# First output product by channels instead of by tokens; the last 64 channels kept as two token halves; x2 split straight from PSUM

## The chip, the cores and the metric

The kernel runs on one core of a Trainium2 chip. The metric is the device time of one execution in microseconds (us): lower is better. The engines are called as in the profile: PE is TensorE (PEld its weight loads), DVE is VectorE, ACT is ScalarE, POOL is GpSimd, SP the engine that issues most DMAs.

## What is computed

```python
# x (2, 4096, 192) f32; weight (8, 7); two pairs w_in (192, 2048), w_out (2048, 192) in f64; a (4), b (2)
w = softmax(weight)                       # per head, over 7 taps
x = causal_conv(x, w)                     # 7 taps along the tokens, head = 24 channels
h = x @ w_in1;  g = h * sigmoid(1.702 * h);  x2 = g @ w_out1
h = x2 @ w_in2
g = (a0 + a1*h + a2*h**2 + a3*h**3) / (1 + |b0|*|h| + |b1|*h**2 + 1e-6)
out = g @ w_out2
```

## The kernel before, in words

The 8192 tokens are 16 blocks of T = 512. Between the two matmul chains every value is channel- or feature-major: partitions are channels, columns are tokens. The 192 channels of a block stand as two tiles of 128 rows: the first 128 channels, and the last 64 channels **twice** (rows 0 to 63 and again 64 to 127), so that two 64-row products can be paired.

f32 products are made of f16 parts: an operand is scaled by a power of two and split into a high and a low half (`high` on ACT, `low` on DVE), and a product is three f16 matmuls (high by high, low by high, high by low). `h_product(m, n, i)` makes 2 x 128 features for 512 tokens of block n and layer m: 6 matmuls of 512 columns over 128 rows (L371) and 6 over 64 rows (L381), which go to two row halves of the array and two PSUM banks in turn. `o1_product` makes x2 = g @ w_out1 **by tokens**: 128 tokens are the stationary operand and 192 channels the columns (L403), 192 matmuls a block. x2 then has to be turned: `x2_natural` copies it from PSUM (ACT, three instructions, L449 and L451), `transposes` turns it on PE (8 times 128x128, L250), DVE takes its maximum (L456), `all_max` spreads that over the partitions with a small matmul (L82), DVE makes a power of two of it (`scales`), and `x2_split` writes the two f16 halves. `o2_chunk` is the last product in f32, 16 chunks a block.

The main loop runs phases j = 0 to 14, written out by hand: each engine executes its instructions in the order of the code. `front_phase` holds, for i = 0 to 7, one `h_product` of layer 1 for block j+1 (followed by GELU on ACT, `g1_high` on POOL, `g1_low` on DVE), one of layer 2 for block j (followed by `unit`: ACT, ACT, DVE, DVE, then `denominator` on DVE), a late `quotient` of block j-1, and two late `o2_chunk`s. `back_phase` holds the transposes of x for block j+3 and its convolution on POOL (`x_conv_pool`: two TENSOR_SCALAR, L297, and one TENSOR_TENSOR, L301, per tap), `o1_product`, the eight logs on ACT, and then what this document calls **the seam**: x2 of block j+1 from PSUM to its f16 halves, beside the inverses (ACT, L502), the first four quotients (DVE, L506) and three chunks of o2. To have work in the seam PE makes the first `h_product` of block j+2 early. PSUM gives three two-bank tiles in turn to the h products, the transposes and the small maxima, and one to each output product.

The 1/(1+q) of the rational function is sigmoid(-ln q), so ACT loads another table three times a phase. The prologue decodes and splits the f64 weights and handles block 0 (its output product in f32, `o1_whole`); blocks 0 to 2 are convolved by matmuls on PE (L286). `last_phase` is the front of block 15 alone.

Of the kernel before, what the change touches and what calls it, by code (L numbers as in the profile page):

```python
# [15 lines left out]
P = 128  # L16
# [4 lines left out]
def kernel(  # L21
# [24 lines left out]
    HALO = K - 1  # L46
    xf = x.rearrange("b s d -> (b s) d")
# [13 lines left out]
    wr = [const.tile([P, 2, DFF // 2], F16, name=f"wr{m}") for m in range(2)]  # L61
# [191 lines left out]

    def x_transpose(n):
        pt = ps_tile("pt")
        transposes(pt, xn_t.pop(n))
        keep = tiny.tile([P, 2, HALO], F32, tag="keep", name="keep")
        if n * T % S == 0:
            nc.gpsimd.memset(keep, 0.0)
            if n:  # L260
                xt_t.pop(n - 1)
        else:
            nc.gpsimd.tensor_copy(out=keep, in_=xt_t.pop(n - 1)[:, :, T:T + HALO])
        t = p1.tile([P, 2, HALO + T], F32, tag="xt", name="xt")
        nc.gpsimd.tensor_copy(out=t[:, :, 0:HALO], in_=keep)
        nc.scalar.activation(out=t[:, :, HALO:HALO + T], in_=pt, func=ACTF.Copy)
        xt_t[n] = t

# [14 lines left out]

    def x_conv_matmul(n, m):
        j, k = m // K, m % K
        nc.tensor.matmul(  # L286
            out=xc_t[n][:, j], lhsT=diag[j, k], rhs=xt_t[n][:, j, k:k + T], start=(k == 0), stop=(k == K - 1)
        )

    def x_conv_pool(n, k):  # L290
        t = xt_t[n]
# [4 lines left out]
        for j in range(2):  # L296
            nc.gpsimd.tensor_scalar(  # L297
                out=d[:, j], in0=t[:, j, k:k + T], scalar1=wt[:, j, k:k + 1], scalar2=1.0, op0=ALU.mult, op1=ALU.mult
            )
        if k:  # L300
            nc.gpsimd.tensor_tensor(out=c, in0=c, in1=d, op=ALU.add)  # L301

    def high(src, s, xs):
        nc.scalar.activation(out=xs[:, 0:2], in_=src, func=ACTF.Identity, scale=s)  # L304

    def low(src, s, xs):
        nc.vector.scalar_tensor_tensor(  # L307
            out=xs[:, 2:4], in0=src, scalar=s, in1=xs[:, 0:2], op0=ALU.mult, op1=ALU.subtract
# [17 lines left out]
    def x_red(n):  # L326
# [3 lines left out]
            out=red[:, 0:1], in_=xn_t[n][:, :, 0:D], axis=AX.XY, op=ALU.max, apply_absolute_value=True  # L330
# [18 lines left out]
    def x_scale_out(n):  # L349
        sc = sc1_t[n]  # L350
        mul(sc[:, 5:6], sc[:, 0:1], cst[:, 2:3])

    def x_high(n):
        xs = xs_t[0, n] = p2.tile([P, 4, T], F16, tag="xs1", name="xs1")
# [6 lines left out]
    def h_product(m, n, i):  # L361

        ph = ps_tile("ph")
        xs = xs_t[m, n]
        terms = ((0, 0), (1, 0), (0, 1))

        def main(first):
            for k in range(2):
                f = slice((NS * k + i) * P, (NS * k + i + 1) * P)
                for q, (a_, b_) in enumerate(terms):  # L370
                    nc.tensor.matmul(  # L371
                        out=ph[:, k], lhsT=wm[m][:, a_, f], rhs=xs[:, 2 * b_], start=(first and q == 0),
                        stop=(not first and q == 2),
                    )

        def rest(first):
            f = slice(i * P, (i + 1) * P)
            for q, (a_, b_) in enumerate(terms):
                for k in range(2):
                    rows = slice(k * D2, (k + 1) * D2)  # L380
                    nc.tensor.matmul(  # L381
                        out=ph[:, k], lhsT=wr[m][rows, a_, f], rhs=xs[rows, 2 * b_ + 1], start=(first and q == 0),
                        stop=(not first and q == 2),
                    )

        for part, first in (((main, True), (rest, False)) if m == 0 else ((rest, True), (main, False))):
            part(first)
        return ph

    po_t, o_done = {}, {}  # L390

    def o_chunk(m, n, f, terms, groups=range(NG)):
# [15 lines left out]
    def o1_product(n, i, hl):  # L408
        for k in range(2):
            f, ts = NS * k + i, slice(k * T, (k + 1) * T)  # L410
            gh, gl, wh, wl = hl[:, 0, ts], hl[:, 1, ts], wo1[:, f, 0:D], wo1[:, f, D:2 * D]
            o_chunk(0, n, f, ((gh, wh), (gh, wl), (gl, wh)))

    def o2_chunk(n, i, k, groups=range(NG)):
        pp = units_t[n][i][0]
        o_chunk(1, n, NS * k + i, ((pp[:, k * T:(k + 1) * T], wo2[:, NS * k + i]),), groups)
# [24 lines left out]
    def x2_natural(n, unit=None):  # L441
        po = po_t.pop((0, n))
        sc = sc1_t.pop(n)
        if unit is None:
            unit = sc[:, 5:6]
        t = p1.tile([P, NG, 2 * P], F32, tag="x2n", name="x2n")
        src = po[:, :, 0:2 * D].rearrange("p k (g d) -> p k g d", g=2)
        dst = t.rearrange("p (k g) d -> p k g d", k=2)
        nc.scalar.activation(out=dst[..., 0:P], in_=src[..., 0:P], func=ACTF.Identity, scale=unit)  # L449
        for c in (P, D):  # L450
            nc.scalar.activation(out=dst[..., c:c + D2], in_=src[..., P:D], func=ACTF.Identity, scale=unit)  # L451
        return t

    def x2_red(t):
        red = tiny.tile([P, 1], F32, tag="red2", name="red2")
        nc.vector.tensor_reduce(out=red, in_=t[:, :, 0:D], axis=AX.XY, op=ALU.max, apply_absolute_value=True)  # L456
        return red
# [8 lines left out]
    def x2_scales(sc):  # L466

        s = sc[:, 2:3]
        mul(s, sc[:, 0:1], cst[:, 3:4])
# [75 lines left out]
    late_pe, early = [], {}  # L545

    def last_phase(j):
# [24 lines left out]
        quotients(range(first))  # L572
        store(j - 1)
        units(first), units(first + 1)
# [13 lines left out]
    def front_phase(j, n1, extras):  # L588

        splits = []  # L590
        for i in range(NS):
            g = gelu(n1, early.pop((n1, i), None) or h_product(0, n1, i))
            hl = g1_high(n1, g)
            splits.append(hl)
            unit(j, h_product(1, j, i))
# [11 lines left out]
    def x2_split(n, pt, sc):  # L607
        xs = xs_t[1, n] = p2.tile([P, 4, T], F16, tag="xs2", name="xs2")
        high(pt, sc[:, 1:2], xs)
        low(pt, sc[:, 1:2], xs)  # L610
        x2_scales(sc)

    def back_phase(j, n1, n2, conv, splits):

        if conv is not None:
            x_transpose(conv)
            for k in range(K):
                x_conv_pool(conv, k)
        for i in range(NS):
            o1_product(n1, i, splits[i])  # L620
            log(j, i)
            if conv is not None and i == 5:
                x_max(conv)
# [208 lines left out]
```

## Time and profile before

| | |
|---|---|
| median of 3 runs | 1261.98 us (1261.32 to 1263.13) |
| the profiled execution: its own time, its span | 1262.34 us, 1260.5 us |
| busy, share of the span: PE, DVE, ACT, POOL | 96%, 84%, 68%, 48% |
| granted TensorE clock, mean | 0.996 of full speed |

A matmul's recorded duration holds its way through the array, which overlaps with the next one's; what a stream of matmuls costs is read from start to start. So "x16, 2.76 us" with a mean of 0.33 us for one is a stream in which one starts every (2.76 - 0.33) / 15 us. An f32 product of 192 columns leaves two records.

### The profile page before, as it was taken

What the parts mean: (1) busy time and instruction counts of PE and PEld (TensorE: products, weight loads), DVE (VectorE), ACT (ScalarE), POOL (GpSimd) and SP (SyncE); (2) the same over time, 40 slices, a digit from 0 to 9 for tenths busy, and PEclk for the clock granted to TensorE, in tenths of its full rate; (3) what the DMA queues carried; (4) which work ended last, traced back from release to release, by engine and by line L of the source; (5) the groups of instructions that cost most, each with busy time, mean ns of one, the idle gap of its engine ahead of it and who ended that gap; (6) DMA issues with size and microseconds to landing.
All of it is one profiled execution on the core that took longest, in us unless ns stands there. A gap on an engine that the chain in (4) does not pass through costs nothing.

```text
span 1260.5 us, 19971 instructions
## 1 busy us (share of the span) xinstructions
PE 1211.6 (96%) x8538; PEld 852.6 (68%) x8538; DVE 1062.8 (84%) x1048; ACT 860.2 (68%) x857; POOL 601.3 (48%) x429
## 2 busy tenths in 40 slices
PE   5899999999999999999999999999999999999997
PEld 2474766768676676867667686766768576686767
DVE  6877889797979979797997979889797988959685
ACT  2624866758586685867668586766858677594975
POOL 2023673928467392755739285572927548101000
PEclk9899999999999999999999999999999999999999
DMA  7700001001010100101010010101001000000000
GB/s 233 234 1 17 1 1 30 1 1 31 1 30 1 30 1 1 30 1 31 1 30 1 1 31 1 30 2 30 1 1 30 1 14 1 14 1 1 14 1 25
DMA packets 31162, 28.56 MB, mean 23 GB/s; under 512 B 9825, under 2 KB 30305, under 8 KB 30305
## 3 DMA queue, kind: packets, MB, share of 16 engines
q1 hardware_dynamic: 30480, 27.27, 7.5%
q8 instruction: 67, 1.10, 0.4%
q14 instruction: 22, 0.18, 0.1%
q10 hardware_dynamic: 593, 0.01, 0.0%
HBM read 20.98 MB, written 6.29 MB: 22 GB/s over the span
## 4 chain that ended last, share of the span: by engine, by line
PE 59%; ACT 20%; DVE 16%; POOL 2%; issue 2%; DMA 1%; ACTq 0%; POOLq 0%; DVEq 0%
PE ph L371 23%; PE po L403 21%; PE ph L381 12%; ACT qq L498 10%; DVE pp L506 6%; PE pc L286 3%; DVE sc L314 3%; ACT qq L502 2%; ACT L502 1%; DVE xs L307 1%; ACT L498 1%; ACT pp L485 1%; ACT xs L304 1%; ACT qq L484 1%; POOL xc L301 1%
## 5 line engine op out<-in xcount | busy, mean ns | idle before, releaser
L431 POOL TENSOR_SCALAR hl<-g,sc 128x1024 f16<-128x1024 f32 x120 | 181.5, 1514 | 460.7 <-ACT g L421 460.6
L371 PE MATMUL ph<-xs,wm 128*128 128x512 f16 x1536 | 375.8, 381 | 3.6 <-ACT xs L304 1.5
L403 PE MATMUL po<-wo,pp 128*128 128x192 f32 x1920 | 334.2, 327 | 18.5 <-DVE pp L506 18.5
L403 PEld LDWEIGHTS po<-wo,pp 128*128 128x128 f32 x1920 | 316.9, 190 | 36.6 <-DVE pp L506 22.1
L403 PE MATMUL po<-wo,hl 128*128 128x192 f16 (+1 forms) x3008 | 265.1, 250 | 5.5 <-ACT on L525 4.2
L371 PEld LDWEIGHTS <-wm 128*128 128x128 f16 x1536 | 139.1, 98 | 191.6 <-issue 62.5
L421 ACT ACTIVATE g<-ph,sc 128x1024 f32<-128x1024 f32 x120 | 133.6, 1113 | 192.1 <-PE ph L381 192.0
L403 PEld LDWEIGHTS <-hl 128*128 128x128 f16 x2880 | 238.5, 98 | 0.8
L506 DVE SCALAR_TENSOR_TENSOR pp<-pp,ab,qq 128x1024 f32<-128x1024 f32 x120 | 201.9, 1692 | 38.0 <-ACT qq L502 38.0
L301 POOL TENSOR_TENSOR xc<-xc,tap 128x1024 f32<-128x1024 f32 x78 | 216.3, 2773 | 6.5
L484 ACT ACTIVATE qq<-ph,sc 128x1024 f32<-128x1024 f32 x128 | 142.4, 1113 | 111.1 <-PE ph L371 100.0
L381 PE MATMUL ph<-xs,wr 64*128 64x512 f16 x1536 | 192.6, 379 | 0.4 <-DVE xs L307 0.4
L437 DVE SCALAR_TENSOR_TENSOR hl<-g,sc,hl 128x1024 f16<-128x1024 f32 x120 | 185.7, 1547 | 1.0 <-POOL hl L431 1.0
L492 DVE SCALAR_TENSOR_TENSOR qq<-qq,ab 128x1024 f32<-128x1024 f32 x128 | 180.7, 1411 | 0.0
L486 DVE TENSOR_TENSOR pp<-pp,ph 128x1024 f32<-128x1024 f32 x120 | 145.3, 1211 | 25.8 <-ACT pp L485 25.8
L487 DVE SCALAR_TENSOR_TENSOR pp<-pp,sc,ph 128x1024 f32<-128x1024 f32 x120 | 153.7, 1281 | 4.3
L498 ACT ACTIVATE qq<-qq,eps,ab 128x1024 f32<-128x1024 f32 x128 | 146.9, 1229 | 1.0 <-DVE qq L492 0.8
L297 POOL TENSOR_SCALAR tap<-xt,wt 128x512 f32<-128x512 f32 x156 | 142.9, 929 | 6.4
L485 ACT ACTIVATE pp<-ph,sc 128x1024 f32<-128x1024 f32 x120 | 143.8, 1198 | 0.0
L381 PEld LDWEIGHTS <-wr 64*128 64x128 f16 x1536 | 63.7, 94 | 117.4 <-issue 61.2
L502 ACT ACTIVATE qq<-qq 128x1024 f32<-128x1024 f32 x128 | 126.2, 1050 | 0.2
L86 DVE TENSOR_REDUCE top<-pm 128x1 f32<-128x128 f32 x35 | 10.0, 286 | 69.5 <-PE pm L82 69.5
(93 smaller groups left out, 702.5 us busy)
## 6 DMA issues: line engine op xcount, KB each, us to landing
xn<-in_x_dram SPq DMA_DIRECT2D x16, 384.0 KB, 4.0
raw<-in_moe_w_out_dram SPq DMA_DIRECT2D x8, 768.0 KB, 7.0
out_dram<-on SPq DMA_DIRECT2D x15, 384.0 KB, 3.0
raw<-in_moe_w_in_dram SPq DMA_DIRECT2D x4, 1024.0 KB, 5.7
xn<-in_x_dram SPq DMA_DIRECT2D x16, 128.0 KB, 4.0
raw<-in_moe_w_in_dram SPq DMA_DIRECT2D x4, 512.0 KB, 7.7
out_dram<-on SPq DMA_DIRECT2D x2, 192.0 KB, 2.0
wt<-in_weight_dram ACTq DMA_DIRECT2D x2, 0.4 KB, 6.5
```

What stands on the lines that cost most here:

```text
L301: nc.gpsimd.tensor_tensor(out=c, in0=c, in1=d, op=ALU.add)
L371: nc.tensor.matmul(out=ph[:, k], lhsT=wm[m][:, a_, f], rhs=xs[:, 2 * b_], start=(first and q == 0), stop=(not first and q == 2),)
L381: nc.tensor.matmul(out=ph[:, k], lhsT=wr[m][rows, a_, f], rhs=xs[rows, 2 * b_ + 1], start=(first and q == 0), stop=(not first and q == 2),)
L403: nc.tensor.matmul(out=dst, lhsT=lhsT[:, g * P:(g + 1) * P], rhs=rhs, start=(done == 0 and g % 2 == 0 and q == 0), stop=(done == NF - 1 an ...
L431: nc.gpsimd.tensor_scalar(out=hl[:, 0], in0=g, scalar1=sc1_t[n][:, 4:5], scalar2=1.0, op0=ALU.mult, op1=ALU.mult)
L437: nc.vector.scalar_tensor_tensor(out=hl[:, 1], in0=g, scalar=sc1_t[n][:, 4:5], in1=hl[:, 0], op0=ALU.mult, op1=ALU.subtract)
L484: nc.scalar.activation(out=qq, in_=h, func=ACTF.Abs, scale=sc[:, 2:3])
L485: nc.scalar.activation(out=pp, in_=h, func=ACTF.Identity, scale=sc[:, 7:8], bias=sc[:, 6:7])
L492: nc.vector.scalar_tensor_tensor(out=qq, in0=qq, scalar=ab[:, 14:15], in1=qq, op0=ALU.add, op1=ALU.mult)
L498: nc.scalar.activation(out=qq, in_=qq, func=ACTF.Ln, scale=ab[:, 15:16], bias=eps)
L502: nc.scalar.activation(out=qq, in_=qq, func=ACTF.Sigmoid, scale=-1.0)
L506: nc.vector.scalar_tensor_tensor(out=pp, in0=pp, scalar=ab[:, 0:1], in1=qq, op0=ALU.add, op1=ALU.mult)
```

## The change

`o1_product` becomes two passes over the block. `o1_main` makes the first 128 channels with the weights as the stationary operand: 48 matmuls of 512 columns. `o1_side` makes the last 64 channels: 96 matmuls of 256 columns with 64 stationary columns, which go in turn to PSUM rows 0 to 63 (first 256 tokens) and 64 to 127 (last 256 tokens). x2 so comes out channel-major in PSUM: the transposes and the copies of x2 are gone, DVE takes the maximum from PSUM, and `x2_split` reads PSUM. The last 64 channels have this form (two token halves on two row halves) everywhere: a block is 768 columns instead of 1024 for `high`, `low`, the convolution and the copies. `h_product` follows: its 12 matmuls of 512 columns become 24 of 256, and the 64-row ones need w_in's last rows a second time with the halves exchanged (`wr[..., 1, ...]`, written by DMAs in the prologue). x is loaded by more and smaller DMAs; the six halo tokens come by DMA and two small matmuls instead of copies on POOL. In `back_phase` all inverses and quotients of the seam are put around it, not into it; two early `h_product`s of layer 1 instead of one are made before x2 is ready, and the first of layer 2 right after it, ahead of the chunks of o2. `x2_scales` (five small DVE instructions) stands between `high` and `low`. In `last_phase` the store stands before the inverses.

```diff
     def x_load(n):
...
+        nc.sync.dma_start(out=t[:, 0:T].rearrange("p (g d) -> p g d", g=NG), in_=src[:, :, 0:P])
+        side = t[:, T:W].rearrange("p (g h d) -> p g h d", g=2, h=2)
+        for h in range(2):
+            nc.sync.dma_start(out=side[:, :, h], in_=src[:, 2 * h:2 * h + 2, P:D])
...
+    def h_main(ph, m, n, i, start=False, stop=False, chunks=range(2)):
+
+        xs = xs_t[m, n]
+        for k in chunks:
+            f = slice((NS * k + i) * P, (NS * k + i + 1) * P)
+            for q, (a_, b_) in enumerate(TERMS):
+                for h in range(2):
+                    nc.tensor.matmul(
+                        out=ph[:, h, k * TH:(k + 1) * TH], lhsT=wm[m][:, a_, f], rhs=xs[:, b_, h * TH:(h + 1) * TH],
+                        start=(start and k == 0 and q == 0), stop=(stop and q == 2), skip_group_check=True,
+                    )
...
+    def o1_main(n, f, terms):
...
+        for q, (w, t, k) in enumerate(terms):
+            nc.tensor.matmul(
+                out=po_t[0, n][:, 0].rearrange("p (h t) -> p h t", h=2), lhsT=w[:, 0:P], rhs=all_tokens(t, k), start=(at == 1 and q == 0),
+                stop=(at == NF and q == len(terms) - 1), skip_group_check=True,
+            )
+
+    def o1_side(n, f, terms):
...
+        for q, (w, t, k) in enumerate(terms):
+            for h in range(2):
+                nc.tensor.matmul(
+                    out=po_t[0, n][h * D2:(h + 1) * D2, 1, 0:TH], lhsT=w[:, P:D], rhs=tokens(t, k, h),
+                    start=(at == 1 and q == 0), stop=(at == NF and q == len(terms) - 1), skip_group_check=True,
+                )
...
+    def x2_split(n, sc, unit):
+        xs = xs_t[1, n] = p2.tile([P, 2, W], F16, tag="xs2", name="xs2")
+        po = po_t.pop((0, n))
+        high(po, sc[:, 1:2], xs)
+        x2_scales(sc, unit)
+        low(po, sc[:, 1:2], xs)
 
     def back_phase(j, n1, n2, conv, splits):
...
+        red = tiny.tile([P, 3], F32, tag="red2", name="red2")
         for i in range(NS):
-            o1_product(n1, i, splits[i])
+            o1_product(o1_main, n1, i, splits[i])
             log(j, i)
...
+        if conv is not None:
+            x_max(conv)
+        x2_red(n1, 0, red)
+        for i in range(NS):
+            o1_product(o1_side, n1, i, splits[i])
...
+        x2_red(n1, 1, red)
+        x2_red_end(red)
...
         if n2 is not None:
...
+            early[n2, 0] = h_product(0, n2, 0, lambda: all_max(red[:, 2:3], pm))
+            early[n2, 1] = h_product(0, n2, 1)
+        else:
+            all_max(red[:, 2:3], pm)
+        each(inverse, j, (0, 1, 2, 3))
         scales(pm, sc)
-        x2_split(n1, pt, sc)
-        each(quotient, j, (2, 3))
+        x2_split(n1, sc, sc1_t.pop(n1)[:, 6:7])
+        each(quotient, j, (0, 1, 2, 3))
         each(inverse, j, (4, 5, 6, 7))
         chunks = [lambda i=i, k=k: o2_chunk(j, i, k) for i in range(NS) for k in range(2)]
+        if n2 is not None:
+            second[n1, 0] = h_product(1, n1, 0)
         for f in chunks[:3]:
             f()
```

How the instructions move at the seam is seen in the order of each engine. First DVE, before, from the first quotient of a back phase to the next two (L506 is a quotient, L456 the maximum of x2, L86 to L319 the power of two, L307 `low`, L314 `x2_scales`):

```order
L506 SCALAR_TENSOR_TENSOR pp<-pp,ab,qq 128x1024
L456 TENSOR_REDUCE red_4005<-x2n 128x1
L506 SCALAR_TENSOR_TENSOR pp<-pp,ab,qq 128x1024
L86 TENSOR_REDUCE top<-pm_3984 128x1
L75 TENSOR_SCALAR sc_4007<-top 128x1
L76 TENSOR_SCALAR sc_4007<-sc_4007 128x1
L319 TENSOR_SCALAR sc_4007<-sc_4007 128x1
L307 SCALAR_TENSOR_TENSOR xs_4025<-pt,sc_4007,xs_4025 128x1024
L314 TENSOR_SCALAR sc_4007<-sc_4007,cst 128x1
L314 TENSOR_SCALAR sc_4007<-ab,sc_4007 128x3
L314 TENSOR_SCALAR sc_4007<-sc_4007 128x2
L314 TENSOR_SCALAR sc_4007<-sc_4007 128x1
```

The same place of DVE in the changed program, where L512 is the maximum of x2, L89 to L348 the power of two, L343 `x2_scales`, L336 `low` and L566 a quotient:

```order
L512 TENSOR_REDUCE red_4589<-po 128x1
L517 TENSOR_SCALAR red_4589<-red_4589 128x1
L89 TENSOR_REDUCE top<-pm_4758 128x1
L78 TENSOR_SCALAR sc_4759<-top 128x1
L79 TENSOR_SCALAR sc_4759<-sc_4759 128x1
L348 TENSOR_SCALAR sc_4759<-sc_4759 128x1
L343 TENSOR_SCALAR sc_4759<-sc_4759,sc_3017 128x1
L343 TENSOR_SCALAR sc_4759<-ab,sc_4759 128x3
L343 TENSOR_SCALAR sc_4759<-sc_4759 128x2
L343 TENSOR_SCALAR sc_4759<-sc_4759 128x1
L336 SCALAR_TENSOR_TENSOR xs_4820<-po,sc_4759,xs_4820 128x768
L566 SCALAR_TENSOR_TENSOR pp<-pp,ab,qq 128x1024 x4
```

No quotient stands in the seam any more, and the four `x2_scales` rows have moved from behind `low` to ahead of it. Then ACT, before, from the table load of the inverses (L502) to the table load of GELU (L449 and L451 are the copies of x2, L304 is `high`):

```order
L502 ACT_TABLE_LOAD
L502 ACTIVATE qq<-qq 128x1024 x2
L449 ACTIVATE x2n<-po,sc_1881 128x4x128
L451 ACTIVATE x2n<-po,sc_1881 128x4x64 x2
L502 ACTIVATE qq<-qq 128x1024 x2
L304 ACTIVATE xs_3344<-pt,sc_3326 128x1024
L502 ACTIVATE qq<-qq 128x1024 x4
L421 ACT_TABLE_LOAD
```

The same place of ACT in the changed program (L562 an inverse, L333 `high`):

```order
L562 ACT_TABLE_LOAD
L562 ACTIVATE qq<-qq 128x1024 x4
L333 ACTIVATE xs_4004<-po,sc_3943 128x768
L562 ACTIVATE qq<-qq 128x1024 x4
L491 ACT_TABLE_LOAD
```

The copies are gone, and four inverses instead of two stand between the table load and the instruction that first needs x2.

## Rows read from the trace of the kernel before

**Rows 1.** The page: busy time by engine, and the clock.

```profile
PE 1211.6 (96%) x8538; PEld 852.6 (68%) x8538; DVE 1062.8 (84%) x1048; ACT 860.2 (68%) x857; POOL 601.3 (48%) x429
...
PEclk9899999999999999999999999999999999999999
```

**Rows 2.** Chain that ended last, one phase: start us, us, what.

```profile
439.19 9.17 ACT qq L498 x8
...
459.88 2.42 DVE sc L314
...
464.18 1.57 PE po L403 x8
...
513.20 9.17 ACT qq L498 x8
```

**Rows 3.** Timeline of that phase's seam: start, us, engine, line, what, [idle before].

```profile
435.43 12.04 PE L403 MATMUL po<-wo,hl 128*128 128x192 f16 x144
...
447.76 0.29 DVE L86 TENSOR_REDUCE top<-pm 128x1 f32<-128x128 f32 x1 [5.00 <-PE pm L82]
...
448.38 1.28 ACT L502 ACT_TABLE_LOAD   x1
...
449.67 2.00 ACT L502 ACTIVATE qq<-qq 128x1024 f32<-128x1024 f32 x2
...
453.66 1.09 PE L250 MATMUL pt<-ident,x2n 128*128 128x128 f32 x8
...
454.78 0.49 PE L82 MATMUL pm<-ident,red 128*128 128x128 f32 x2
...
457.01 1.11 ACT L304 ACTIVATE xs<-pt,sc 128x1024 f16<-128x1024 f32 x1 [1.99 <-DVE sc L319]
...
458.16 1.28 DVE L307 SCALAR_TENSOR_TENSOR xs<-pt,sc,xs 128x1024 f16<-128x1024 f32 x1 [1.24 <-ACT xs L304]
...
459.91 2.35 POOL L301 TENSOR_TENSOR xc<-xc,tap 128x1024 f32<-128x1024 f32 x1
...
464.18 1.57 PE L403 MATMUL po<-wo,pp 128*128 128x192 f32 x8 [1.56 <-DVE pp L506]
```

**Rows 4.** Timeline of PE in one step of a front.

```profile
404.97 1.46 PE L371 MATMUL ph<-xs,wm 128*128 128x512 f16 x6
...
406.36 1.47 PE L381 MATMUL ph<-xs,wr 64*128 64x512 f16 x12
...
409.07 2.76 PE L403 MATMUL po<-wo,pp 128*128 128x192 f32 x16
```

**Rows 5.** A front by window: length, then busy of PE, PEld, DVE, ACT, POOL.

```profile
466.45:516.78 50.33, 50.33 (x351) 33.47 (x350) 50.03 (x38) 30.83 (x30) 19.30 (x16) 1.00 0.07 19
```

**Rows 6.** Groups by line: count, busy us, mean ns, idle before.

```profile
L403 PEld LDWEIGHTS <-hl 128*128 128x128 f16 x2880 | 238.5, 98 | 0.8
...
L301 POOL TENSOR_TENSOR xc<-xc,tap 128x1024 f32<-128x1024 f32 x78 | 216.3, 2773 | 6.5
...
L250 PEld LDWEIGHTS pt<-ident,xn 128*128 128x128 f32 x128 | 15.2, 146 | 10.0 <-issue 6.9 <-DMA xn<-in_x_dram 1.6 <-PE ph L371 0.8
...
L456 DVE TENSOR_REDUCE red<-x2n 128x1 f32<-128x768 f32 x16 | 15.1, 943 | 1.6 <-ACT x2n L451 1.6
```

**Rows 7.** Timeline of the prologue and of the last two blocks.

```profile
58.03 9.65 PE L403 MATMUL po<-v,hl 128*128 128x192 f32 x48
...
82.02 10.47 PE L286 MATMUL pc<-xt,diag 128*128 128x512 f32 x24
...
1183.79 3.71 PE L403 MATMUL po<-wo,hl 128*128 128x192 f16 x43
...
1194.06 0.82 PE L381 MATMUL ph<-xs,wr 64*128 64x512 f16 x6
...
1230.34 4.28 PE L403 MATMUL po<-wo,hl 128*128 128x192 f32 x16 [4.23 <-ACT on L525]
```

**Rows 8.** One stretch of that end by window, columns as in rows 5, then the clock.

```profile
1230.34:1233.40 3.06, 3.06 (x10) 3.06 (x11) 2.49 (x3) 3.06 (x4) 0.00 (x0) 0.52 0.40 129
```

More of the change, by code (lines that the diff above doesn't have):

```diff
@@ L266, in x_transpose, with turn, halo @@
-        nc.scalar.activation(out=t[:, :, HALO:HALO + T], in_=pt, func=ACTF.Copy)
+        src, b = xn_t.pop(n), hn[n % 2]
+        def turn(dst, a_, cols):
+            nc.tensor.transpose(out=dst, in_=a_, identity=ident[:, 0:cols])
+        def halo(dst, a_):
+            nc.tensor.matmul(out=dst, lhsT=a_, rhs=ident[:, 0:HALO], start=True, stop=True, skip_group_check=True)
+        halo(pt[:, 0, 0:HALO], b[:, P:2 * P])
+        halo(pt[:, 0, HALO + TH:2 * HALO + TH], b[:, 0:P])
+        for g in range(2):
+            turn(pt[:, 0, HALO + g * P:HALO + (g + 1) * P], src[:, T + g * P:T + (g + 1) * P], P)
@@ L358, in x_low @@
         low(xc_t.pop(n), sc1_t[n][:, 1:2], xs_t[0, n])
-    def h_product(m, n, i):
-        ph = ps_tile("ph")
[L364 to L387, printed above, removed]
-        return ph
+    TERMS = ((0, 0), (1, 0), (0, 1))
@@ new lines, in h_side @@
+    def h_side(ph, m, n, i, start=False, stop=False):
+        xs = xs_t[m, n]
+        f = slice(i * P, (i + 1) * P)
+        for other in range(2):
+            for q, (a_, b_) in enumerate(TERMS):
+                for h in range(2):
+                    rows, k = slice(h * D2, (h + 1) * D2), h ^ other
+                    nc.tensor.matmul(
+                        out=ph[:, h, k * TH:(k + 1) * TH], lhsT=wr[m][rows, a_, other, f], rhs=xs[rows, b_, T:W],
+                        start=(start and other == 0 and q == 0), stop=(stop and q == 2), skip_group_check=True,
+                    )
@@ new lines, in h_product, with tokens, all_tokens @@
+    def h_product(m, n, i, between=None):
+        ph = ps_tile("ph")
+        at = (ph, m, n, i)
+        if m:
+            h_side(*at, start=True)
+            h_main(*at, stop=True)
+        else:
+            h_main(*at, start=True, chunks=(0,))
+            if between is not None:
+                between()
+            h_main(*at, chunks=(1,))
+            h_side(*at, stop=True)
+        return ph
+    def tokens(t, k, h):
+        return t[:, h * T + k * TH:h * T + (k + 1) * TH]
+    def all_tokens(t, k):
+        return t.rearrange("p (h k t) -> p h k t", h=2, k=2)[:, :, k]
@@ L439, in g1_low, with x2_red, x2_red_end @@
         )
[L441 to L457, printed above, removed]
+    def x2_red(n, j, red):
+        nc.vector.tensor_reduce(
+            out=red[:, j:j + 1], in_=part_of(po_t[0, n], j), axis=AX.X, op=ALU.max, apply_absolute_value=True
+        )
+    def x2_red_end(red):
+        nc.vector.tensor_scalar(out=red[:, 2:3], in0=red[:, 0:1], scalar1=red[:, 1:2], scalar2=None, op0=ALU.max)
     def b_consts():
@@ L571, in last_phase @@
         units(first - 1, len(late_pe))
-        quotients(range(first))
+        each(log, j, range(first))
         store(j - 1)
+        for i in range(first):
+            inverse(j, i)
+            quotient(j, i)
         units(first), units(first + 1)
@@ L719, in o1_whole @@
                 w = val_t["out", 0, f // 4].bitcast(F32)[:, f % 4 * D:(f % 4 + 1) * D]
-                o_chunk(0, 0, f, ((g0[i][:, k * T:(k + 1) * T], w),))
+                for part in (o1_main, o1_side):
+                    part(0, f, ((w, g0[i], k),))
         flat = wo2.rearrange("p f d -> p (f d)")
```

149 lines of the change are left out of this document (80 added, 69 removed).

## The prediction

> **What bounds the kernel now.** I read the page first: PE is busy for 96% of the span, at full clock in all but the first slices [rows 1]. Then the chain of work that ended last: it repeats every 74.02 us (439.19 to 513.20), and in each period it leaves PE once, for the seam, where DVE waits in a two-element instruction of `x2_scales` for 2.42 us and a quotient follows late, before PE goes on with a chunk of o2 [rows 2]. The timeline of the seam shows the cost: PE stands still for 1.56 us ahead of that chunk [rows 3]; start to start it is 1.72. A window over a front says what is next: in 50.33 us PE has no gap, and DVE is busy for 50.03 of them [rows 5]. So a phase is a stream of PE work with one stall, and DVE is full in the front and has its idle time in the back, 5.00 us in one piece while it waits for a small maximum [rows 3]. A change pays if it takes columns off PE or that stall away, and only as far as DVE follows.
>
> **What a matmul costs here.** Start to start: f16 matmul of 512 columns (1.46 - 0.38) / 5 = 0.216 us; a pair on two row halves (1.47 - 0.38) / 5 = 0.218, so both run at once; a 192-column one of o1 (12.04 - 0.25) / 143 = 0.0825 [rows 3, 4]. These are columns / 2.4 GHz plus 2.5 ns. For 256 columns I take 0.109. A weight load shows 98 ns but keeps a pace of 0.0825 in o1 [rows 3, 6], so it hides behind 0.109. Going from the full array to a row half or back costs 0.09 (the first L381 stands 0.31 behind the last L371 start) [rows 4].
>
> **The change on PE, per phase.**
> 1. `o1_product`: 192 x 0.0825 = 15.86 goes. `o1_main` is 48 x 0.216 = 10.36. `o1_side` is 48 pairs on two column halves. The trace has no such pair. From below a pair costs one matmul, 0.109; from above two in turn, 0.218. The nearest row is the pair on row halves, which runs at the price of one [rows 4], so I take 0.109: 5.25, and two changes of mode 0.19. Sum -0.06. The columns are the same in number; without overlap the term is +5.2.
> 2. `h_product`: 192 matmuls of 256 columns for 96 of 512, and 96 half-array pairs for 48: +0.36.
> 3. The transposes of x2 go. From their first to the small maximum behind them PE spends 453.66 to 454.78 [rows 3], and a further 0.1 on the product's restart: -1.22.
> 4. x: 6 transposes instead of 8, -0.22; two halo products of six columns are bound by their four f32 weight loads, at most the 0.11 that a transpose's takes start to start: +0.44. Sum +0.2.
> 5. The stall of 1.72 at the chunk, with 0.1 behind it: -1.82. The quotients have time now, see below.
> 6. New waits at the seam, counted from the start S of o1. `o1_side` ends at S + 15.9. DVE's maximum of the last 256 columns is 0.42 (0.29 for 128 and 0.94 for 768 give 1.03 ns a column [rows 3, 6]), then one small instruction, 0.2: the small matmul can start at S + 16.8. PE has half an `h_product` for that, 0.65 us: wait 0.15. ACT has its four inverses done at 448.38 + 1.28 + 4 x 1.0 = S + 18.2; the scale is ready at the same time; `high` is 1.11 x 3/4 = 0.85, to S + 19.1; `low` 1.28 x 3/4 = 0.98 [rows 3]. PE meanwhile has the rest of two `h_product`s, to S + 20.65. If `x2_scales` takes 0.8 (four instructions of 0.2), `low` ends at S + 20.2: no wait.
> But the two-element instruction now stands ahead of `low`. In the row it took 2.42 us and ended with a TENSOR_TENSOR of POOL that ran 459.91 to 462.26 [rows 2, 3]; the convolution is still on POOL at S + 18.6. Bounds: no wait, or the 2.35 us of that row's instruction, of which PE feels 1.7. POOL's instructions shrink by a quarter, so the whole one would be 1.8, and on average I meet one half way: PE feels about 0.6. I take 0.6.
> Sum: -0.06 + 0.36 - 1.22 + 0.2 - 1.82 + 0.15 + 0.6 = **-1.8 per phase**, 72.2 instead of 74.0.
>
> The Trainium skill, SBUF — State Buffer, section Who interferes with whom, says that DVE in a two-port mode and GpSimd share a port pair as an exclusive lock for the whole instruction, the later one blocked until the end. By that rule a TENSOR_SCALAR of POOL can block it as well as a TENSOR_TENSOR, and the term would stay between 0 and 1.7; the row agrees, no run here shows the two apart.
>
> **Why the quotients and DVE don't hold it up.** `low` done at S + 20.2 to 22, four quotients of 1.3 to 1.66 end by S + 28.3; the first chunk of o2 starts at S + 22.7 behind the first `h_product` of layer 2 and needs only the first quotient. The next front starts on DVE with its first `unit`, which waits for ACT: `high`, four inverses, table load, GELU and two more ACT instructions, S + 28 against S + 31.0 before. DVE then needs the same 50 us less 0.3 for the shorter `low` of x, so it ends 3 us earlier relative to S, and PE's 2 us come out of it. DVE's margin is small: its slack in the front is 0.3 us of 50 [rows 5].
>
> **Sum over the run.** 13 phases with a convolution: -23.4. The one without (no stall now, none after): -0.6. Prologue: the convolution on PE is 7 x 512 + 7 x 256 columns instead of 14 x 512, a quarter less; for block 1 it is alone on the path (10.47 for 12 of 14 matmuls [rows 7]): -3.0. `o1_whole` alternates full and half array for each of its 16 pieces, 32 x 0.09 = 3.0 us, of which about 1.1 lies on the path (three of its eight steps stand ahead of a scale that DVE waits for), and block 0's `high` and first product come about 0.5 earlier: together -2.4. Front of phase 0, where block 2 is convolved between the products: -3.0 on PE, of which I keep 1.3, since DVE ends that front late.
> The end loses. With no block left, no early product stands in the seam of phase 14, and its quotients wait behind `low`. Before, o1 ended at 1187.50 and three chunks of o2 filled the time to the next `h_product` at 1194.06, 6.56 later [rows 7]. Now `low` ends 4.25 behind o1, the first quotient 5.55, three chunks of 1.3 follow: 9.45, +2.9. PE idles for 4.4 us there; after 4.23 idle us at 1230.34 its clock fell to the lower level, 1.2 GHz, 0.52 on average over 3.06 us [rows 7, 8], which cost 1.5, so I add 1.3. From there PE sets the pace to the logs of the last block: +4.0 with o1's gain taken off. The store moved ahead of the inverses changes nothing: ACT does the same work before it takes up the next unit.
> -23.4 - 0.6 - 2.4 - 1.3 + 4.0 = -23.7. From the profiled execution's 1262.34 (span 1260.5 and 1.84 around it) that is 1238.6; the median of the runs shown is 0.36 below the profiled one: **1238 us**.
>
> **Rivals.**
> - *The halves run in turn* (slower). Against: a row-half pair overlaps. For: another axis of the array, two moving streams of 128 rows each, no row of it. Then o1_side is 10.5: +5.2 in 15 phases, +78.6, and about 4 in the prologue: 1321. It needs less: -23.7 over 15 x 48 pairs is 33 ns, so from 0.142 us a pair the change is no gain. Chance 0.20 with what lies between the two prices, 0.02 of it under 0.142.
> The Trainium skill, TensorEngine Tiling (Array Packing), section Tile-to-Partition Mapping, says that column tiling switches off the fast weight load. An f32 load of 128 columns reads 146 ns against 98 for f16, and transposes still start every 0.11 us behind such loads [rows 6]; two 64-column loads one after the other at that rate make about 0.11 a pair, just hidden, and if each took 0.11, 0.22 a pair: 1321 again. No run here has shown it.
> - *The port wait in full* at `low`: 1.7 instead of 0.6, 13 x 1.1 = +14: 1252. For: 2.42 us in the row of before. Against: it met the longest kind of POOL instruction at its start. Chance 0.13.
> - *No port wait*: 13 x 0.6 less, 1230. Chance 0.16.
> - *DVE takes over*: PE gets ahead, the PSUM tiles come back no sooner than DVE reads them, and a phase stays within 0.5 us of 74.0: 1256 to 1262. For: 50.03 of 50.33 busy. Against: its 3 us earlier start. Chance 0.10, of which 0.06 within 0.2% of no change (2.5 us, about what a measurement here can tell).
> - My forecast, 1238 give or take 7: 0.41.
>
> **Range and chances.** The rivals on the fast side lie at 1230, below them I leave 1 in 20: 1226. Above, 1252 and the DVE case are in, and most of the halves case is out: 1262. That leaves out 0.18 above and some 0.03 below. Faster by more than 0.2%: 0.41 + 0.13 + 0.16 + 0.04 + 0.02 = 0.76; same 0.06; slower 0.18.
>
> **What would show it.** The side matmuls: pairs about 0.109 apart, or 0.218. At the seam: whether `x2_scales` has a row of 1 to 2 us that ends with a POOL instruction, and whether the first layer-2 product waits for `low`. Period of the logs near 72.2. In the last seam an idle PE of 4 us and a lower clock behind it. Wrong it would be if a column pair costs over 0.14, or if the front shows PE gaps that end with DVE's reads of PSUM.

## The result and the profile after

The changed kernel takes **1273.2 us** (median of 7 runs, 1266.0 to 1274.9), the kernel before 1262.1 (1261.0 to 1263.1): ratio 1.0084, 95% interval 1.0065 to 1.0103. It is slower; the forecast was 1238 and faster. Six of the seven runs lie between 1273.0 and 1274.9; the profiled one is the shortest (1266.0, span 1264.0). A second profile of the same kernel (below, span 1273.1) is of the common kind. The two differ by 8.1 us at the start; behind it they agree to 1 us, which lies at the end.

The chain that ended last, over one seam of the first profile (start us, us, what), answers to [rows 2]:

```profile
429.98 10.36 PE po L463 x48
440.34 0.23 PE pm L85 x2
...
441.30 0.15 DVE sc L348
441.46 0.61 DVE red L512
442.07 0.04 issue
442.11 5.43 PE po L473 x96
447.54 0.76 PE ph L400 x6
...
451.08 0.92 DVE xs L336
452.00 2.77 DVE pp L566
454.77 0.14 issue
454.90 6.74 PE po L452 x40
```

Before, the chain left PE once in a period, for the seam's scaling. Now it leaves PE ahead of `o1_side` (L473) as well, for a maximum that DVE takes of `o1_main`'s sums (L512). The timeline of the same seam, with what each engine waited for in brackets, answers to [rows 3]:

```profile
440.18 0.39 PE L85 MATMUL pm<-ident,red 128*128 128x128 f32 x2
441.37 0.68 DVE L512 TENSOR_REDUCE red<-po 128x1 f32<-128x512 f32 x1
442.11 5.43 PE L473 MATMUL po<-hl,wo 128*64 128x256 f16 x96 [1.55 <-DVE red L512]
442.44 1.28 ACT L562 ACT_TABLE_LOAD   x1
448.31 0.49 PE L85 MATMUL pm<-ident,red 128*128 128x128 f32 x2
448.73 1.80 POOL L330 TENSOR_TENSOR xc<-xc,tap 128x768 f32<-128x768 f32 x1
449.84 0.71 DVE L343 TENSOR_SCALAR sc<-ab,sc 128x3 f32<-128x3 f32 x1
450.59 0.48 DVE L343 TENSOR_SCALAR sc<-sc 128x2 f32<-128x2 f32 x2
450.99 1.01 DVE L336 SCALAR_TENSOR_TENSOR xs<-po,sc,xs 128x768 f16<-128x768 f32 x1
451.86 1.82 POOL L330 TENSOR_TENSOR xc<-xc,tap 128x768 f32<-128x768 f32 x1
451.92 6.43 DVE L566 SCALAR_TENSOR_TENSOR pp<-pp,ab,qq 128x1024 f32<-128x1024 f32 x4
454.90 6.74 PE L452 MATMUL po<-wo,pp 128*128 128x192 f32 x40 [0.44 <-DVE pp L566]
516.50 1.28 ACT L562 ACT_TABLE_LOAD   x1
```

The period is 516.50 - 442.44 = 74.06 us, as before. PE waits 1.55 for L512, and the view of waits has 21.6 us of it in 15 phases: 13 of this size and 0.78 in each of the last two, which have no convolution and so no small instructions ahead of L512. From the last matmul of `o1_main` to the first of `o1_side` it is 2.14 us start to start; in the two edited kernels below, where `o1_side` doesn't wait, it is 0.53, so the wait costs 1.61 a phase. The 96 side matmuls take 5.43, one of them 0.27, so a pair of column halves is (5.43 - 0.27) / 47 = 0.110 start to start. The old stall of 1.56 at the chunk is 0.44. And of the four quotients, which sum to 6.43, the first takes 2.84: POOL's TENSOR_TENSOR started 0.06 us ahead of it. The front behind the seam has no gap, and DVE is less full than in [rows 5] (length; then busy time and instructions of PE, PEld, DVE, ACT, POOL; granted clock; DMA):

```profile
454.90:503.80 48.90, 48.90 (x450) 43.23 (x451) 46.07 (x36) 27.38 (x27) 18.59 (x8) 1.00 0.05 14
```

Where the time lies in the run, cut at ACT's table loads for the logs of phases 0 and 14:

| stretch | before | forecast | second profile after | first profile after |
|---|---|---|---|---|
| start to phase 0's back | 143.08 | -3.7 | 143.57 (+0.5) | 135.45 (-7.6) |
| to phase 14's back | 1030.84 | -24.0 | 1033.64 (+2.8) | 1033.64 (+2.8) |
| to the end | 86.63 | +4.0 | 95.85 (+9.2) | 94.90 (+8.3) |

The end, in the first profile, answers to [rows 7] and [rows 8]; the last line is a window, with the clock ahead of the last two numbers:

```profile
1177.97 5.43 PE L473 MATMUL po<-hl,wo 128*64 128x256 f16 x96 [0.78 <-DVE red L512]
...
1188.93 6.09 PE L452 MATMUL po<-wo,pp 128*128 128x192 f32 x24 [4.28 <-DVE pp L566]
1194.95 0.83 PE L413 MATMUL ph<-xs,wr 64*128 64x256 f16 x12
...
1228.96 2.84 PE L452 MATMUL po<-wo,hl 128*128 128x192 f32 x16 [1.80 <-DVE hl L566]
...
1249.55 10.40 PE L452 MATMUL po<-wo,hl 128*128 128x192 f32 x48 [5.16 <-DVE hl L566]
```
```profile
1249.55:1260.00 10.45, 10.40 (x48) 10.10 (x48) 2.33 (x2) 0.53 (x2) 0.00 (x0) 0.77 0.00 0
```

The last 48 matmuls before the change:

```profile
1248.45 8.07 PE L403 MATMUL po<-wo,hl 128*128 128x192 f32 x48 [1.27 <-DVE hl L506]
```

PE stands idle for 4.28 us in the seam and for 5.16 ahead of the last 48 matmuls, which then take 10.40 instead of 8.07, at a granted clock of 0.77 on average, between the two levels of 1.2 and 2.4 GHz. Behind the idle stretch of the seam, 24 matmuls take 6.09 at a granted clock of 0.67; in the kernel before they took 4.07.

### The profile page after: what moved, and what is told of

Its sections match the earlier page's. It is cut to its first block, busy times and chain, and to the rows that moved or that the text cites. A ratio compares the mean times of both kernels' runs of the same rounds, so it can differ in the third digit from the quotient of the medians.

```text
span 1264.0 us, 24525 instructions
## 1 busy us (share of the span) xinstructions
PE 1204.1 (95%) x10762; PEld 959.3 (76%) x10762; DVE 1049.3 (83%) x1095; ACT 828.0 (66%) x825; POOL 495.7 (39%) x400
## 4 chain that ended last, share of the span: by engine, by line
PE 84%; DVE 12%; ACT 2%; issue 2%; DMA 1%; ACTq 0%; DVEq 0%
PE po L452 25%; PE ph L400 23%; PE po L463 13%; PE ph L413 12%; PE po L473 7%; DVE pp L566 3%; DVE sc L343 1%; PE pc L316 1%; DVE xs L336 1%; PE pm L85 1%; DVE v L167 1%; DVE red L512 1%; PE pt L270 1%; DVE v L176 1%; DVE top L89 1%
## 5 line engine op out<-in xcount | busy, mean ns | idle before, releaser
L501 POOL TENSOR_SCALAR hl<-g,sc 128x1024 f16<-128x1024 f32 x120 | 210.8, 1756 | 540.1 <-ACT g L491 540.1
L400 PE MATMUL ph<-xs,wm 128*128 128x256 f16 x3072 | 382.2, 274 | 3.5 <-ACT xs L333 2.2
L400 PEld LDWEIGHTS <-wm 128*128 128x128 f16 x3072 | 287.3, 98 | 75.2 <-issue 38.4
L413 PE MATMUL ph<-xs,wr 64*128 64x256 f16 x3072 | 194.6, 271 | 0.8 <-DVE xs L336 0.8
L566 DVE SCALAR_TENSOR_TENSOR pp<-pp,ab,qq 128x1024 f32<-128x1024 f32 x120 | 179.5, 1525 | 0.0
L413 PEld LDWEIGHTS <-wr 64*128 64x128 f16 x3072 | 138.1, 94 | 47.4 <-issue 33.0
L463 PE MATMUL po<-hl,wo 128*128 128x512 f16 x720 | 157.8, 379 | 0.0
L330 POOL TENSOR_TENSOR xc<-xc,tap 128x768 f32<-128x768 f32 x78 | 152.6, 1956 | 6.5
L463 PEld LDWEIGHTS <-wo 128*128 128x128 f16 x720 | 70.3, 98 | 81.7
L562 ACT ACTIVATE qq<-qq 128x1024 f32<-128x1024 f32 x128 | 124.5, 1046 | 0.2
L326 POOL TENSOR_SCALAR tap<-xt,wt 128x512 f32<-128x512 f32 (+1 forms) x156 | 101.4, 662 | 6.4
L473 PE MATMUL po<-hl,wo 128*64 128x256 f16 x1440 | 81.5, 273 | 21.6 <-DVE red L512 21.6
```

Source lines behind the costliest of these rows:

```text
L330: nc.gpsimd.tensor_tensor(out=flat_of(c), in0=flat_of(c), in1=flat_of(d), op=ALU.add)
L400: nc.tensor.matmul(out=ph[:, h, k * TH:(k + 1) * TH], lhsT=wm[m][:, a_, f], rhs=xs[:, b_, h * TH:(h + 1) * TH], start=(start and k == 0 an ...
L413: nc.tensor.matmul(out=ph[:, h, k * TH:(k + 1) * TH], lhsT=wr[m][rows, a_, other, f], rhs=xs[rows, b_, T:W], start=(start and other == 0 a ...
L463: nc.tensor.matmul(out=po_t[0, n][:, 0].rearrange("p (h t) -> p h t", h=2), lhsT=w[:, 0:P], rhs=all_tokens(t, k), start=(at == 1 and q == ...
L473: nc.tensor.matmul(out=po_t[0, n][h * D2:(h + 1) * D2, 1, 0:TH], lhsT=w[:, P:D], rhs=tokens(t, k, h), start=(at == 1 and q == 0), stop=(at ...
L501: nc.gpsimd.tensor_scalar(out=hl[:, 0], in0=g, scalar1=sc1_t[n][:, 4:5], scalar2=1.0, op0=ALU.mult, op1=ALU.mult)
```

## The experiments

Intervals are of the ratio to the kernel before. Stretches "to the end" are counted from the logs' table load of phase 14, as in the table. Each edit is made to the changed kernel; ... marks what is left out of an edit.

**The changed kernel again, unedited** (1275.0, one run).

> The changed kernel once more, unedited. Its profiled execution took 1266.0 us, six timed ones 1273.0 to 1274.9. If the difference of 7 us is spread over the phases (another position of the convolution on POOL against DVE's instructions of the seam), a second profile that falls near 1273 shows a period of the logs' table loads of about 74.5 instead of 74.06 us. If it lies in one place (the load of x and the weights, or the end), the period is 74.06 again and one stretch is 7 us longer. If the profile falls near 1266 again, the profiler itself goes with the shorter time and nothing is told apart.

The period is 74.06 again; one place is longer, the start. DVE's timeline, first of the earlier profile, then of this one:

```profile
10.88 0.16 DVE L114 TENSOR_REDUCE mx<-wt 128x2 f32<-128x14 f32 x1
```
```profile
17.41 0.17 DVE L114 TENSOR_REDUCE mx<-wt 128x2 f32<-128x14 f32 x1 [6.19 <-DMA ab<-in_moe_b_dram]
```

The softmax of the taps waits for small loads, which ACT issues (queue q10). The queues' rows (packets, MB, share of 16 engines) of the window 12 to 18 us, here, show q10 still busy beside the weights' loads on q1:

```profile
q1 hardware_dynamic: 551, 1.53, 99.1%
q10 hardware_dynamic: 231, 0.00, 3.6%
```

The first profile has 185 packets of q10 in this window too, and no wait: what differs is whose they are. By the packets' sizes and times in the two traces, the taps' packets, of 28 bytes, end at 9.68 us there and at 16.61 here. Those of b, of 8 bytes, end at 18.01 here, behind the start of the softmax; so it is the taps that it waits for, though the view names b. Of the ten profiles of kernels with this order of loads, nine start the softmax between 17.25 and 17.67 us and the first alone at 10.88.

In the kernel before the same window holds no packet of q10. SP then issued its first two weight loads from 1.77 to 9.25 us; now, behind more loads of x and the halo, it issues four between 3.64 and 6.71.

**One maximum behind `o1_side`** (1254.4; 0.9946, 0.9929 to 0.9963) and **two tiles** (1255.4; 0.9950, 0.9935 to 0.9965): two ways to take the wait ahead of `o1_side` away.

```
-        x2_red(n1, 0, red)
         for i in range(NS):
             o1_product(o1_side, n1, i, splits[i])
...
-        x2_red(n1, 1, red)
-        x2_red_end(red)
+        nc.vector.tensor_reduce(
+            out=red[:, 2:3], in_=flat_of(po_t[0, n1]), axis=AX.X, op=ALU.max, apply_absolute_value=True
+        )
```
```
+    def pair():
+        return [ps_o.tile([P, 512], F32, tag=f"o{k}", name=f"po{k}") for k in range(2)]
...
-            po_t[0, n] = ps_o.tile([P, 2, 512], F32, tag="o", name="po")
+            po_t[0, n] = pair()
...
```

> One maximum over all 768 columns behind o1_side in place of one of 512 ahead of it and one of 256 behind it, so that o1_side's first matmul waits for no DVE instruction. Theory A (PE sets the pace; the missed wait of 1.71 us per phase ate the gain): the wait goes, the maximum behind o1_side is longer by 0.94 - (0.42 + 0.04 + 0.21) = 0.27, so -1.4 us in each of 15 phases, -21 us, about 1252 against 1273; period 72.6. Rival B (DVE sets the pace of a phase, the wait only stands in time that PE would lose anyway): the time comes back as gaps ahead of products or at the chunk, 1270 to 1274, period 74.0.

> The sums of o1_main and o1_side in two tiles of one bank each, so that the maximum of the first may run beside o1_side; high and low are two instructions each. Theory A: the wait of 1.71 goes, low ends some 0.3 later against PE (second instructions of high and low), of which the chunk's wait grows; -1.4 us in 15 phases, about 1252; period 72.6. Rival B (DVE sets the pace): 1270 to 1276, since DVE has one instruction more.

Theory A, twice: 18.8 and 17.8 us less (21 were expected), a period of 72.75 and 72.87. The seam with one maximum, then `o1_side` and the first maximum (L522) with two tiles:

```profile
586.92 5.43 PE L473 MATMUL po<-hl,wo 128*64 128x256 f16 x96
...
592.39 0.96 DVE L701 TENSOR_REDUCE red<-po 128x1 f32<-128x768 f32 x1 [3.89 <-PE po L473]
593.40 0.49 PE L85 MATMUL pm<-ident,red 128*128 128x128 f32 x2 [0.29 <-DVE red L701]
...
595.16 1.81 POOL L330 TENSOR_TENSOR xc<-xc,tap 128x768 f32<-128x768 f32 x1
595.21 2.04 DVE L343 TENSOR_SCALAR sc<-sc 128x2 f32<-128x2 f32 x2
...
597.16 1.01 DVE L336 SCALAR_TENSOR_TENSOR xs<-po,sc,xs 128x768 f16<-128x768 f32 x1
598.23 0.61 PE L413 MATMUL ph<-xs,wr 64*128 64x256 f16 x8 [0.52 <-DVE xs L336]
```
```profile
587.97 5.43 PE L483 MATMUL po<-hl,wo 128*64 128x256 f16 x96
...
588.85 0.68 DVE L522 TENSOR_REDUCE red<-po 128x1 f32<-128x512 f32 x1
```

In both `o1_side` follows at once; with two tiles the maximum runs beside it. Since the seam now falls elsewhere against POOL's convolution, two tiny instructions of `x2_scales` take 2.04 us where they took 0.48, and PE waits 0.52 for `low` (0.92 with two tiles, where `high` and `low` are two instructions each).

**The first quotient early** (1271.5; 1.0079, 1.0064 to 1.0095).

```
+        inverse(j, 0)
+        quotient(j, 0)
         x2_red(n1, 1, red)
...
-        each(inverse, j, (0, 1, 2, 3))
+        each(inverse, j, (1, 2, 3))
...
-        each(quotient, j, (0, 1, 2, 3))
+        each(quotient, j, (1, 2, 3))
```

> The first quotient moved from behind low into DVE's idle time of 4.9 us beside o1_side; the wait of o1_side stays. Theory A: only the chunk's wait for that quotient goes (0.61 + 0.07 in 13 phases): -8 us, about 1265. Rival B (DVE sets the pace): 1.3 to 2.8 us of DVE's work leaves the busy part of each phase, -17 to -36 us, 1237 to 1256.

Neither: 1.6 us. The chunk no longer waits, but PE now waits 0.4 us for `low` in 12 phases. POOL and DVE beside `o1_side`:

```profile
599.43 2.11 POOL L326 TENSOR_SCALAR tap<-xt,wt 128x512 f32<-128x512 f32 x2
599.90 1.29 DVE L566 SCALAR_TENSOR_TENSOR pp<-pp,ab,qq 128x1024 f32<-128x1024 f32 x1 [2.16 <-ACT qq L562]
```

The early quotient (1.29 us) held POOL's second TENSOR_SCALAR, whose row has 2.11 for 1.15, so POOL's sums came later and met other DVE instructions. A wait on this pair is moved, not removed, by moving one side.

**POOL cut short** (1246.8; 0.9879, 0.9864 to 0.9893) and **POOL's sums in three** (1247.5; 0.9885, 0.9871 to 0.9900), both with one maximum.

```
-            for k in range(K):
+            for k in range(K - 2):
                 x_conv_pool(conv, k)
...
```
```
-            nc.gpsimd.tensor_tensor(out=flat_of(c), in0=flat_of(c), in1=flat_of(d), op=ALU.add)
+            for q in range(3):
+                s = slice(q * TH, (q + 1) * TH)
+                nc.gpsimd.tensor_tensor(out=flat_of(c)[:, s], in0=flat_of(c)[:, s], in1=flat_of(d)[:, s], op=ALU.add)
...
```

> The kernel with one maximum, and the last two taps of POOL's convolution left out (the two are missing from the output of 13 blocks), so that POOL's last TENSOR_TENSOR ends ahead of the seam's scaling instead of beside it. In the kernel with one maximum the two-element instruction of x2_scales takes 2.04 us for 0.48 and ends with such an instruction; PE waits 0.5 for low in 12 phases. Theory A (DVE is held by POOL): the row is 0.48 again, the quotients 4 x 1.2, PE's wait for low goes: -0.5 to -0.7 in 13 phases, 1246 to 1248 against 1254. Rival B (DVE waits there for ACT's high or for its own queue): 1254.

> The kernel with one maximum, and each sum of POOL's convolution (768 columns, 1.81 us) in three instructions of 256 columns. Theory A (DVE is held until the end of POOL's two-input instruction that runs at the time): the most that one DVE instruction is held falls from 1.8 to some 0.65 us; x2_scales' row of 2.04 becomes 0.5 to 1.1, PE's wait for low (0.5 in 12 phases) goes: -6 us, 1247 to 1249 against 1254, if POOL's overheads don't push the convolution past the quotients. Rival B (DVE and POOL share by turns, so the sum of what DVE loses is the same however it is cut): 1253 to 1256.

Both come out as theory A has it, 7.7 and 6.9 us less. The timeline with POOL cut short, then with its sums in three:

```profile
591.27 0.48 DVE L343 TENSOR_SCALAR sc<-sc 128x2 f32<-128x2 f32 x2
...
592.82 4.87 DVE L566 SCALAR_TENSOR_TENSOR pp<-pp,ab,qq 128x1024 f32<-128x1024 f32 x4
```
```profile
592.69 0.63 DVE L345 TENSOR_SCALAR sc<-ab,sc 128x3 f32<-128x3 f32 x1
...
593.35 0.67 DVE L345 TENSOR_SCALAR sc<-sc 128x2 f32<-128x2 f32 x2
...
594.86 6.08 DVE L568 SCALAR_TENSOR_TENSOR pp<-pp,ab,qq 128x1024 f32<-128x1024 f32 x4
```

The 2.04 falls to 0.48 without POOL's work, and to 0.67 with it in short pieces. The four quotients still lose 1.2 us with short pieces (6.08 against 4.87), but PE doesn't wait for them. The period is 72.06 in both.

**The taps' loads ahead of the weights'** (1269.6; 1.0062, 1.0047 to 1.0077).

```
+            queue = (nc.scalar, nc.sync)[k]
-            nc.scalar.dma_start(out=wt[p0:p0 + first, 1], in_=weight[full:full + 1].to_broadcast([first, K]))
-            nc.scalar.dma_start(
+            queue.dma_start(out=wt[p0:p0 + first, 1], in_=weight[full:full + 1].to_broadcast([first, K]))
+            queue.dma_start(
                 out=wt[p0 + first:p0 + D2, 1],
...
```

> The changed kernel with two of the six loads of the convolution's weights issued by SP, ahead of the loads of the weight matrices. In the second profile of the changed kernel DVE's softmax of the taps waited 6.2 us for these small loads and started at 17.41 us, in the first at 10.88, and everything behind it stood 6.5 to 8.1 us later. Theory A (the small packets take turns with those of the weights, which now are issued at 3.64 to 6.7 us instead of in two goes until 10.5): the softmax starts near 11, a second table load near 31 instead of 36.7, -6 us: about 1267 in every run. Rival B (the wait is for something else, the loads of a and b or a slow queue of the chip in these runs): no change, 1273.

Theory A, in part: phase 0's back starts at 138.16 instead of 143.57, and DVE doesn't wait for the taps. From median to median it is 3.5 us of the 6. The start still lies 2.7 behind the first profile's 135.45: the first weight load now lands later, and DVE starts on it at 11.73 instead of 9.01.

**The last seam rearranged** (1271.4; 1.0075, 1.0060 to 1.0090).

```
+        if n2 is None:
+            inverse(j, 0)
+            quotient(j, 0)
         x2_red(n1, 1, red)
...
-        if n2 is not None:
-            second[n1, 0] = h_product(1, n1, 0)
+        second[n1, 0] = h_product(1, n1, 0)
+        if n2 is None:
+            second[n1, 1] = h_product(1, n1, 1)
```

> The changed kernel with its last seam alone rearranged: the first quotient into DVE's idle time beside o1_side, and two products of layer 2 ahead of the chunks of o2. Theory A (the end lost 8.3 us against the kernel before: first product of layer 2 5.9 later behind o1, and a last stretch of chunks at the lower clock): that product starts 7 us earlier, ACT's and DVE's chain of the last block with it, of which 3 to 6 us come through: 1267 to 1270. Rival B (the end is set by ACT's and DVE's work from the last low on, whatever PE does first): 1272 to 1274.

The stretch to the end is 92.5 instead of 95.85, 3.3 less, the least that A allows; the first product of layer 2 came 9 us earlier behind o1's start, so most of its lead is lost again. From median to median 1.8 us are left, 1271.4, between the ranges of A and B.

**The store put back** (1273.0; 1.0088, 1.0073 to 1.0103) and **PE kept busy** (1271.7; 1.0078, 1.0061 to 1.0094).

```
-        each(log, j, range(first))
+        quotients(range(first))
         store(j - 1)
-        for i in range(first):
-            inverse(j, i)
-            quotient(j, i)
```
```
         quotients(range(first, NS))
+        ph = ps_tile("ph")
+        for m in range(20):
+            nc.tensor.matmul(
+                out=ph[:, 0], lhsT=wm[1][:, 0, 0:P], rhs=xs_t[1, j][:, 0, 0:T], start=(m == 0), stop=(m == 19)
+            )
```

> The changed kernel with the order of before at the end: the store of the last block but one behind the five inverses and quotients instead of ahead of them. The prediction held that the place of the store is worth nothing. Theory A (the end is set by ACT's and DVE's chain, so the 2 us that PE's chunks gain from the early store only lengthen PE's gap ahead of the last 48 matmuls from 1.27 to 5.16 us, behind which they run at the lower clock, 10.42 us for 8.07): the gap is about 3 shorter, the last 48 take 8.1, -2 us: 1271. Rival B (the gap stays long enough for the lower clock, or the clock falls for another reason): 1273 to 1275.

> The changed kernel with 20 matmuls of 512 columns whose sums are not used, ahead of the last three units' chunks, where PE stands idle for 5.2 us. Theory A (idle PE loses the clock): the last 48 matmuls take 8.1 instead of 10.4 us, -2.3 us: about 1271. Rival B (the last 48 are slow for another reason, their data or the stores): 1273 or more, the 48 still 10.4.

PE's timeline, first with the store put back, then with PE kept busy:

```profile
1240.59 5.49 PE L452 MATMUL po<-wo,hl 128*128 128x192 f32 x16 [4.18 <-ACT on L585]
...
1259.34 8.07 PE L452 MATMUL po<-wo,hl 128*128 128x192 f32 x48 [0.63 <-DVE hl L566]
```
```profile
1253.81 4.48 PE L645 MATMUL ph<-xs,wm 128*128 128x512 f16 x20
1259.14 8.07 PE L452 MATMUL po<-wo,hl 128*128 128x192 f32 x48 [0.85 <-DVE hl L566]
```

In both the 48 take 8.07: what is idle ahead of them sets their pace, not their data. With the store back, the idle stretch and the slow matmuls only stand earlier (4.18 us, then 5.49 for 2.84). The stretch to the end is 92.8 and 92.9 instead of 95.85; the phases ahead, which the edits don't touch, were 1 to 1.6 us longer in these two profiles, so the times can't show a gain of this size.

**Three places together** (one maximum, last seam, taps: 1249.2; 0.9902, 0.9885 to 0.9918) and **all** (with POOL's sums in three and PE kept busy: **1238.2**; 0.9816, 0.9802 to 0.9830).

> One maximum, the last seam rearranged and the taps' loads split, together. If the three are separate places, the gains add up: 1254 - 6 - 3 to 6 = 1242 to 1245, 1.3% faster than the kernel before. If one of them only makes room for a wait elsewhere, 1248 or more.

> All the places together: one maximum, POOL's sums in three instructions, the last seam rearranged, the taps' loads split, and 20 unused matmuls in PE's last gap. One maximum and the sums in three gave 1247.5. If the rest adds up: -4 to -5 for the taps, -3.3 for the last seam, -2 for the clock, 1237 to 1238, which is also the time that was predicted for the change. If the last seam gives nothing beside one maximum, as the sum of three places suggests (1249.2 where 1244 was expected), 1240 to 1242.

The three miss their sum: to the end they need 93.65, one maximum alone 93.49. The seam itself is shorter, but PE's last gap is 5.16 us with and without, and the 48 behind it took 10.76 and 10.12. With PE kept busy they take 8.07, and the sum comes out: 1238.2, where 1237 to 1238 was expected.

## Why the prediction was wrong

**The step that failed is the timing under 6**, "`o1_side` ends at S + 15.9" (measured: 447.54 - 429.82, S + 17.7): it takes `o1_side` to start right behind `o1_main`. In the program the maximum of the first sums is issued ahead of `o1_side`, and both sums are parts of one tile `po`; so the program lets the first side matmul wait for DVE, though it writes other columns of the tile than DVE reads. The listing of PE's program order with its waits has it:

```
L473 MATMUL po<-hl_822,wo_82 64x256 [waits DVE_49]
```

Behind `o1_main` come a small matmul, a maximum of 128, three tiny instructions and the maximum of 512: a wait that costs 1.61 us in 13 phases and 0.85 in two, 22.6 us in all. The prediction costed the second maximum and its wait (0.15; measured 0.17) and didn't ask who waits for the first. With two tiles nothing waits there, with the maximum in the same place of the program; that the shared tile makes the wait is thereby shown.

The other steps:

- *1, column pairs* (0.109): right, 0.110. The rival of halves in turn is out.
- *2 to 4, products, transposes*: not shown one by one, right in sum to 0.2: 74.06 less 1.61 and the 0.68 that the chunk waits start to start is 71.8; 72.2 less the port wait's 0.6 is 71.6. The kernel with one maximum and POOL cut short bears the two prices out: its period of 72.06 is 74.06 less both, with 0.29 for the longer maximum.
- *5, the stall at the chunk*: "The quotients have time now" was too much. The old stall went (it stood in 12 phases, not in the 13 that the sum takes it out of; phase 0 before is 72.73 long), but the first quotient is held for 1.57 us (2.84 for 1.27), and PE waits 0.44 for it.
- *6, the port wait*: right in kind and size, wrong in place: 0.68 at the chunk behind the quotient instead of 0.6 at `low`. With one maximum it stood exactly where it was forecast, 2.04 us in `x2_scales` and 0.52 on PE. The Trainium skill, SBUF — State Buffer, section Who interferes with whom, says too that a DVE instruction with two SBUF inputs contends with a POOL instruction that reads SBUF, and that one with at most one and no two-port mode doesn't. The trace agrees: the quotient, with both inputs in SBUF, was held; `low`, which reads x2 from PSUM, took 1.01 us, also in the 11 phases with POOL's sums in three in which it started inside one of them.
- *DVE takes over*: didn't happen. Both edits that freed PE of the wait brought the time down, and the front stays without gaps on PE.
- *The prologue* (-2.4, phase 0 -1.3): right that work there shrinks, -7.6 in the first profile. Not foreseen: in nine of ten profiles the softmax waits for the taps' small packets, +8.1, so that +0.5 is left. That it comes of SP issuing the weights at other times, behind the added loads of x and the halo, is argued from the order of issues; shown is that the wait goes when two of the taps' loads are issued ahead of the weights. The Trainium skill, DMA: Bandwidth & Descriptors, section Queues, rings and completion order, says that a DMA engine takes turns between queues packet by packet; the two queues' packets in one window agree with it, and no run here shows the turns themselves. Why the first profile escaped stays open.
- *The end* (+4.0): the seam right in kind and too small, the last 48 matmuls not foreseen; +9.2, in the first profile +8.3. There the first product of layer 2 came 5.9 us later behind o1's start (+2.9 forecast, and 1.3 for the clock): `o1_side`'s wait stands there too (0.78 idle), and 24 matmuls behind the idle stretch took 2.0 longer. The lower clock cost 2.3 more at the last 48. That the store moved ahead "changes nothing" holds for the time (1273.0 with it put back), within what these runs can tell; in the trace it moves PE's idle stretch to the last place, and the stretch to the end is 3.1 shorter with it put back.

Added up against the second profile (12.5 us above the kernel before, 36.2 above the forecast of -23.7): the wait in 14 phases 13 x 1.61 + 0.85 = 21.8, the start 4.2, the end 5.2. Of the 5.0 left, 1.3 is phase 0, which before was that much shorter than the period the sum takes; the rest, some 0.3 a phase, was not followed further.

With the wait and POOL's long pieces gone, the 14 phases take 1006.8 us, 24.0 less than before, which is the forecast for them. That is in part luck: 13 x 0.6 = 7.8 us of port wait stand in the forecast and aren't paid there, and as much is lost elsewhere, above all in the longer maximum, in the 0.2 a phase above, and in phase 0. That the last kernel takes 1238.2, the forecast time, is luck too: it has edits that the change lacks.

## What to carry to other kernels

When a sum is split into two passes so that the next engine can begin on the first part, the second pass can wait for that reader, as it did here, where the program keeps both parts in one tile; give each part its own tile, or read both at the end, and look for the wait in the program's list of waits before costing anything.

A wait between DVE and POOL is a matter of phase: an edit that shifts the seam by a microsecond moves it to another instruction. Shorter POOL instructions bound it wherever it falls.

A small load beside large ones at the start can land late: look at which queue's packets are still on the way when the first consumer waits.

## What the runs showed of the hardware that was not expected

- Two streams of 256 columns through two column halves of the array cost 0.110 us a pair, what one of 256 columns takes start to start, with weight loads of 64 columns hidden (48 pairs in 5.43 us).
- DVE and POOL hold each other: a POOL TENSOR_TENSOR of 1.81 us held a two-element DVE instruction to its end, and a DVE quotient held a POOL TENSOR_SCALAR (2.11 for 1.15).
- Idle stretches of 4.18 to 5.16 us on PE were followed by slower f32 matmuls (10.40 instead of 8.07 for 48, at a granted clock of 0.77); 20 matmuls put into the idle stretch kept the pace, and an idle stretch moved elsewhere took the slow matmuls with it.
